# Two first expert products behind attention, later row turning, copies ahead of a square, another pair order

## The chip, the cores and the metric

The kernel runs on one core of a Trainium2 chip. The metric is the device time of one execution in microseconds (us), the median of several runs. The core has a matrix engine (TensorE, PE in the views; its weight loads are PEld), a vector engine (VectorE, DVE), a scalar engine (ScalarE, ACT), GpSimd (POOL), and SyncE (SP), which here does nothing but issue DMAs. Each engine executes its own instructions in order; engines meet through semaphores.

## What is computed

Attention without softmax over 8 batches of 2496 tokens, then a mixture of 8 experts, where each token goes to one expert and an expert keeps the 80 tokens of largest gate weight:

```python
scores = (1.0 / S) * np.matmul(z, z.transpose(0, 2, 1))   # z: 8 x 2496 x 64
attn = np.maximum(scores, 0.0) ** 2
x = u * np.matmul(attn, v)                                # u, v: 8 x 2496 x 256
logits = x.reshape(-1, 256) @ w_gate                      # 256 x 8
expert_idx = argmax(logits); gate_w = softmax(logits)[expert_idx]
for e in range(8):                                        # at most 80 tokens each
    h = np.maximum(x[tok_idx] @ w1[e], 0.0)               # w1: 256 x 1024
    out[tok_idx] = gate_w[tok_idx, None] * (h @ w2[e])    # w2: 1024 x 256
```

## The kernel before

**Tiles and stages.** Attention runs batch by batch. A batch has 5 chunks of queries (`qc` 0 to 4, 512 columns, the last 448) and 20 blocks of 128 keys, taken in 10 pairs. A step is one chunk with one pair (`r` 0 to 9 counts the steps of a chunk), so there are 8 x 5 x 10 steps. Products are made in two-part precision: a number is a high part (`ah`, a cast) and a low part (`al`, the difference, L58). A step has 24 accumulating products (L444, `acc`), and most of them also 6 score products (L407, `s`).

**Look ahead.** In step i the scores of step i+2 are issued: PE writes `s`, ACT takes the positive part (L409) and the square (L410), ACT or DVE casts `ah`, DVE makes `al` (L58). Scores are symmetric, so a block below the diagonal is not computed again: DVE turns it (L316, `x`), SP writes it to DRAM (L326, `y`) and later reads it back as `blk` (L343); then ACT casts it (L387) and DVE makes its `al`. Four slots hold such blocks. The diagonal's quarter goes the same way through `xd`, `yd` and `md`. The tables `pairs_of`, from `order()`, say in which order a chunk takes its pairs. In chunk 3 that is pair 6, 0, 8, 9, 1, 2, 3, 4, 5, 7; pairs 6 to 9 are scored, 0 to 5 are read back.

**The chain of a finished chunk.** When the ten pairs are summed in the two accumulators, `take` copies them (ACT, L516). In the steps of the following chunk DVE adds the first part of it (`chunk_add`, r=0), multiplies with `u` (`chunk_x`, L524, r=1), takes the rest (`chunk_rest`, r=3) and the low part (`chunk_lo`, tile `xl`, r=5); a store at r=4 (`chunk_store`), the gate logits (L602) at r=7 and their sum (L609) at r=8 end it. `CHAIN` holds these numbers. All of it stands in the same queues as the attention work of the next chunk.

**Rows for the experts.** The experts read tokens as rows, and `x` is kept as columns. In batches 0 and 1 each finished chunk is turned at once by two DMA transposes (L560) and written as rows (L568); from batch 2 on the chunk is stored to DRAM as it is (`xu`, L580).

**The end.** Behind the last chunk PE makes the first product of expert 0 (`first_product`, `hp_first`, L832), a count of tokens (`count`, L711), and the logits of the last chunk (L549, L553). The last `x` of attention is finished by `chunk_x_last` (ACT copies L538, DVE). Then each expert's products follow: `hp` (L832), the transposes `tp` (L1351), `op` (L1366). The experts' weights are split in high and low parts by ACT and DVE casts and subtractions (L911, L921), the first of them at the steps listed in `SPLITS`.

**What sets the order.** The program is issued in the written order under a manual schedule: the position of a call in the loop over the steps is the position in every engine's queue. SP issues all the DMAs of the loop, and a DMA that waits for its source or for a free slot holds everything behind it.

Of the kernel before, what the change touches and what calls it, by code (L numbers as in the profile page):

```python
# [25 lines left out]
def attn_moe_kernel(ctx, tc, zT, uT, v, wg, w1, w2, out, seq, cap):  # L26
# [30 lines left out]
    def tt(o, a, b, op):  # L57
        V.tensor_tensor(out=o, in0=a, in1=b, op=op)  # L58
# [36 lines left out]
    gt = dram.tile([NTOK, 1], F32, name="gt")  # L95
    xu = {(b, qc): dram.tile([P, DC, CH], F32, name=f"xu_{b}_{qc}") for b in range(2, B) for qc in range(NQ)}

# [293 lines left out]

    def scores(b, qc, k):
# [17 lines left out]
        nc.scalar.activation(out=a[:, :, c0:c1], in_=a[:, :, c0:c1], func=AF.Square)  # L410
        return lambda: split(b, qc, k, a, diag, lower, c0, nq)
# [86 lines left out]
    def top(x):  # L498
        return x.bitcast(BF16)[..., 1::2]

    def chunk_tiles(b, qc):
        xf = xpool.tile([P, 2, DC, CH], F32, tag="xf", name=f"xf_{b}_{qc}")

        xl = xpool.tile([P, DC, CH], BF16, tag="xl", name=f"xl_{b}_{qc}")
        nq = min(CH, seq - qc * CH)
        xt_t[b, qc] = [x[..., :nq] for x in (xf[:, 0], xf[:, 1], xl)]
        return xf[..., :nq]
# [67 lines left out]
    def chunk_store(b, qc):  # L575

        xf = xt_t[b, qc][0]
        nq = min(CH, seq - qc * CH)
        if b >= 2:
            nc.sync.dma_start(out=xu[b, qc][:, :, :nq], in_=xf)  # L580
        elif qc in (2, 3):
            xq = sqpool.tile([P, 2, QT * 2 * D], U16, tag="x", name=f"xq_{b}_{qc}")[:, 0]
            xq_t[b, qc] = x_turn(xf, xq, nq)
        else:
            xq = zpool.tile([P, QT * 2 * D], U16, tag="vraw", name=f"xq_{b}_{qc}", bufs=3)
            xq_t[b, qc] = x_turn(xf, xq, nq)

    def chunk_store2(b, qc):
        if b < 2:
            x_rows(b, qc, min(CH, seq - qc * CH), xq_t.pop((b, qc)))  # L590
# [394 lines left out]
    def weights_ahead(qc, r):  # L985
        if not places:
# [72 lines left out]
    ex_t = {}  # L1059
    CHAIN = 3, 5, 4, 6, 7, 8  # L1060

    with tc.manual_schedule(engines={ET.PE, ET.Activation, ET.DVE, ET.SP, ET.Pool}):
# [10 lines left out]
        for i, (b, qc, r) in enumerate(steps):  # L1073
# [239 lines left out]
    def ffn_of(own, num, expert, tw, to, ps_t, ps_h):  # L1313
# [66 lines left out]
    def ahead():  # L1380
        with ExitStack() as stack:
# [58 lines left out]
            with tc.manual_schedule(engines={ET.PE, ET.Activation, ET.DVE, ET.Pool}):  # L1440
# [3 lines left out]
                for i in range(E):  # L1444
# [7 lines left out]
                    if i + 1 < E:  # L1452
                        ffn_x(i + 1, xall[0][:, i + 1], V)
# [96 lines left out]
    with tc.If(nc.values_load(flag[0:1, 0:1], min_val=0, max_val=1) > 0):  # L1550
        for i in range(B * NQ):
            zero_out(i, B * NQ)
        with tc.tile_pool(name="gx", bufs=1) as gx:
# [55 lines left out]
```

## Time and profile before

| | us |
|---|---|
| median of 3 runs | 1342.36 (1341.12 to 1347.63) |
| the profiled execution | 1343.44 |
| its span in the trace | 1341.7 |
| PE busy | 1304.5 |
| DVE busy | 1060.9 |
| ACT busy | 1014.0 |
| share of the 16 DMA engines, main queue | 76.0% |

Names in the rows carry the program's names without buffer numbers. A timeline row is one or several like instructions of an engine that follow each other (`x4`): when the first began, how long from there to the end of the last, and in brackets how long the engine had been idle before and what released it. In the rows of a window, busy times stand with the number of instructions. Matmuls overlap, so that between two of full width that wait for nothing some 0.23 us pass from start to start although each is listed with 0.39.

Batches 3 to 7 take about 157 us each, from the first accumulating product of one to that of the next; batches 1 and 2 take 159.

### The profile page before, as it was taken

The numbers are of one execution on the slowest core, as the hardware profiler recorded it, in microseconds if no ns is written. First come the engines' busy times: TensorE is split into PE (matmuls) and PEld (weight loads), VectorE is DVE, ScalarE is ACT, GpSimd is POOL, SyncE is SP. The second block draws the span as 40 slices with busy tenths as digits, with TensorE's granted clock in tenths as the row PEclk, the third lists the DMA queues.
The fourth block names the chain that finished last, engine by engine and source line by source line (L and its number), as shares of the span: only waits on it lengthen the run. The fifth ranks groups of instructions, "written<-read, shape, count | busy, mean of one in ns | idle before, by whom it ended". The sixth has DMA issues, their size and how long they took to land.

```text
span 1341.7 us, 31268 instructions
## 1 busy us (share of the span) xinstructions
PE 1304.5 (97%) x13119; PEld 1071.5 (80%) x13119; DVE 1060.9 (79%) x1277; ACT 1014.0 (76%) x1102; POOL 43.3 (3%) x58
## 2 busy tenths in 40 slices
PE   9999899999999999999999999999999999999997
PEld 6887778778877788878888788887888788887886
DVE  7877698677887788787887688877887778877785
ACT  8976688766887578776887678876787768878765
POOL 0000000000001000000002000000000000003011
PEclk9999999999999999999999999999999999999989
DMA  6798978987877848969578877788579695689763
GB/s 209 255 285 246 244 225 245 266 235 223 256 242 228 242 156 244 277 189 267 163 236 251 247 206 219 225 262 229 164 237 262 200 264 168 216 252 260 220 217 120
DMA packets 192740, 306.98 MB, mean 229 GB/s; under 512 B 35872, under 2 KB 117712, under 8 KB 182352
## 3 DMA queue, kind: packets, MB, share of 16 engines
q1 hardware_dynamic: 191312, 302.62, 76.0%
q0 software_dynamic: 1280, 2.30, 0.6%
q8 instruction: 104, 1.70, 0.5%
q14 instruction: 44, 0.36, 0.1%
HBM read 163.66 MB, written 136.09 MB: 223 GB/s over the span
## 4 chain that ended last, share of the span: by engine, by line
PE 72%; DVE 8%; ACT 7%; DMA 7%; issue 4%; SPq 2%; POOL 0%; DVEq 0%; ACTq 0%; POOLq 0%
PE acc L444 57%; PE s L407 9%; DVE al L58 3%; DMA blk<-y 2%; ACT a L409 2%; DVE x L316 2%; ACT ah L114 2%; PE hp L832 1%; PE pl L602 1%; DMA md<-yd 1%; ACT a L410 1%; PE op L1366 1%; DMA zraw<-zT 1%; DVE xf L58 1%; ACT ah L387 1%
## 5 line engine op out<-in xcount | busy, mean ns | idle before, releaser
L444 PE MATMUL acc<-ah,vt 64*128 64x512 f32 (+1 forms) x6240 | 954.7, 383 | 5.7 <-ACT xf L516 5.3
L444 PEld LDWEIGHTS acc<-ah,vt 64*128 64x128 f32 x6240 | 586.7, 184 | 121.2 <-ACT xf L516 14.9
L444 PE MATMUL acc<-al,vt 64*128 64x512 f32 (+1 forms) x3120 | 614.4, 385 | 17.1 <-DVE al L58 16.5
L58 DVE TENSOR_TENSOR al<-a,ah 128x1024 fp32r<-128x1024 f32 (+1 forms) x240 | 271.0, 1129 | 143.9 <-ACT ah L114 141.2
L444 PEld LDWEIGHTS acc<-al,vt 64*128 64x128 f32 x3120 | 300.0, 184 | 86.8 <-DVE al L58 33.5
L409 ACT ACTIVATE a<-s 128x1024 f32<-128x1024 f32 x240 | 229.2, 955 | 137.8 <-PE s L407 112.9
L410 ACT ACTIVATE a<-a 128x1024 f32<-128x1024 f32 x240 | 238.1, 992 | 7.6
L387 ACT CAST ah<-blk 128x1024 fp32r<-128x1024 f32 x160 | 164.5, 1050 | 99.5 <-PE acc L444 93.2
L58 DVE TENSOR_TENSOR al<-blk,ah 128x1024 fp32r<-128x1024 f32 x160 | 193.6, 1221 | 46.5 <-ACT ah L387 43.8
L114 ACT CAST ah<-a 128x1024 fp32r<-128x1024 f32 (+3 forms) x217 | 213.4, 984 | 5.7
L316 DVE STREAM_TRANSPOSE x<-a 128x1024 f32<-128x1024 f32 x160 | 198.1, 1238 | 0.0
L58 DVE TENSOR_TENSOR xf<-xf 128x1024 f32<-128x1024 f32 (+1 forms) x78 | 91.9, 1178 | 0.0
L407 PE MATMUL s<-zh,zl 64*128 64x512 f32 x480 | 89.8, 371 | 0.0
L407 PE MATMUL s<-zl,zh 64*128 64x512 f32 x480 | 89.7, 370 | 0.0
L516 ACT COPY xf<-acc 128x1024 f32<-128x1024 f32 (+1 forms) x78 | 76.4, 994 | 15.0 <-PE acc L444 14.3
L407 PE MATMUL s<-zh,zh 64*128 64x512 f32 x320 | 63.4, 393 | 0.0
L58 DVE TENSOR_TENSOR al<-md,ah 128x512 fp32r<-128x512 f32 x37 | 25.1, 679 | 35.2 <-ACT ah L422 35.1
L407 PEld LDWEIGHTS s<-zl,zh 64*128 64x128 f32 x480 | 45.2, 185 | 8.4
L407 PEld LDWEIGHTS s<-zh,zl 64*128 64x128 f32 x480 | 45.4, 185 | 6.4
L147 DVE TENSOR_TENSOR vt<-vraw,vt 128x1024 fp32r<-128x1024 f32 x40 | 48.5, 1213 | 0.0
L524 DVE SCALAR_TENSOR_TENSOR xf<-xf,ut 128x1024 f32<-128x1024 f32 (+1 forms) x39 | 45.8, 1175 | 0.0
L58 DVE TENSOR_TENSOR xl<-xf 128x1024 bf16<-128x1024 f32 (+1 forms) x39 | 45.8, 1174 | 0.0
(190 smaller groups left out, 738.5 us busy)
## 6 DMA issues: line engine op xcount, KB each, us to landing
y<-x SPq DMA_DIRECT2D x80, 1024.0 KB
blk<-y SPq DMA_DIRECT2D x320, 256.0 KB
out<-idle SPq DMA_DIRECT2D x40, 512.0 KB
vraw<-v SPq DMA_DIRECT2D x32, 512.0 KB
ut<-uT SPq DMA_DIRECT2D x32, 512.0 KB
wraw<-w SPq DMA_DIRECT2D x30, 512.0 KB
xu<-xf SPq DMA_DIRECT2D x24, 512.0 KB
yd<-xd SPq DMA_DIRECT2D x37, 256.0 KB
```

The costliest lines, as they stand in the source:

```text
L58: V.tensor_tensor(out=o, in0=a, in1=b, op=op)
L114: eng.copy(out=o, in_=i)
L147: e1.tensor_tensor(out=vt[:, :, 1], in0=raw, in1=vt[:, :, 0], op=ALU.subtract)
L316: V.transpose(out=x[:, :, :, t:t + 2].rearrange("p n k t s -> p t k n s"), in_=a)
L387: nc.scalar.copy(out=natural(ah), in_=src)
L407: nc.tensor.matmul(s[:, h, c0:c1], zk[hs, t * P:(t + 1) * P], zq[hs], start=n == 0, stop=n == 2)
L409: nc.scalar.activation(out=a[:, :, c0:c1], in_=s[:, :, c0:c1], func=AF.Relu)
L410: nc.scalar.activation(out=a[:, :, c0:c1], in_=a[:, :, c0:c1], func=AF.Square)
L444: nc.tensor.matmul(acc_t[b, qc][c][:, h, :nq], v_t[b, k // QT][hs, k % QT, iv, c * P:(c + 1) * P], x[hs, k % 2, :nq], start=at not in begu ...
L516: nc.scalar.copy(out=x[:, :, c], in_=acc_t[b, qc][c][:, :, :x.shape[-1]])
L524: V.scalar_tensor_tensor(out=x[:, 0], in0=x[:, 0], scalar=CSQ, in1=u_t[b, qc][:, :, :x.shape[-1]], op0=ALU.mult, op1=ALU.mult)
L602: nc.tensor.matmul(to[:, h, t], xb[i % 3][hs, i // 3, t0:t0 + P], wgs[hs, i // 3], start=i == 0, stop=i == 3 * DC - 1)
```

## The change

Six edits are made together.

1. All chunks are stored to `xu`. Those of batches 0 and 1 are turned later: in chunks 0 and 1 of batches 2 to 6, one stored chunk each is loaded (r=1), turned by the same two DMA transposes (r=4) and written as rows (r=7), in buffers of `vraw`.
2. Chunk 3 takes its pairs in the order 6, 0, 1, 8, 9, 2, 3, 4, 5, 7.
3. At the last step of a batch the square of the pair scored there is issued behind the two copies of the finished chunk.
4. The low part of `x` is written into the low halves of the rest's own words; the tile `xl` goes.
5. In chunk 0 of a batch the chain of the finished chunk begins one step later (add at r=1, product with `u` at r=2, rest at r=4).
6. Behind attention the first products of experts 0 and 1 are made in a row (`hp_first`, `hp_second`), ahead of the logits and the count. The splits of expert 1's last weights move from steps 4, 5 and 6 of the last chunk to 6, 8 and 9.

```diff
-            rest = rest[:1] + rest[-2:] + rest[1:-2]
+            rest = rest[:2] + rest[-2:] + rest[2:-2]
...
+        if later:
+            return lambda: (square(), split(b, qc, k, a, diag, lower, c0, nq))
+        square()
...
-        tt(xl, xr, top(xr), ALU.subtract)
+        tt(xr.bitcast(BF16)[..., 0::2], xr, top(xr), ALU.subtract)
...
+        nc.sync.dma_start(out=xu[b, qc][:, :, :min(CH, seq - qc * CH)], in_=xf)
...
+    def turn(step):
+        b, qc = to_turn[0]
         nq = min(CH, seq - qc * CH)
-        if b >= 2:
-            nc.sync.dma_start(out=xu[b, qc][:, :, :nq], in_=xf)
...
+        if step == 0:
+            xt_t["turn"] = x = raw_tile(f"xt_{b}_{qc}")
+            nc.sync.dma_start(out=x[:, :, :nq], in_=xu[b, qc][:, :, :nq])
+        elif step == 1:
+            xq = raw_tile(f"xq_{b}_{qc}").rearrange("p c t -> p (c t)").bitcast(U16)
+            xq_t["turn"] = x_turn(xt_t.pop("turn"), xq, nq)
         else:
...
+            to_turn.pop(0)
+            x_rows(b, qc, nq, xq_t.pop("turn"))
...
+    def first_products():
...
+        x_t[1] = x_second
+        nc.scalar.copy(out=x_t[1][0], in_=xp[:, :DC * NS])
+        tt(x_t[1][1], xp[:, :DC * NS], x_t[1][0], ALU.subtract)
         hp = ps_s.tile([P, 2, CH], F32, tag="s", name="hp_first")
...
+        hp = ps_a.tile([P, 2, CH], F32, tag="acc", name="hp_second")
+        for part in range(2):
+            product1(hp[:, part], 1, 1, part, NS)
...
-    SPLITS = dict(zip([(qb, 2), (qb, 4), (qb, 6), (qb, 7), (qz, 2), (qz, 4), (qz, 5), (qz, 6)], early))
+    SPLITS = dict(zip([(qb, 2), (qb, 4), (qb, 6), (qb, 7), (qz, 2), (qz, 6), (qz, 8), (qz, 9)], early))
...
-                rest = scores(nb, nqc, 2 * pairs_of[nb, nqc][nr])
+                rest = scores(nb, nqc, 2 * pairs_of[nb, nqc][nr], r == NP - 1 and qc == NQ - 1)
...
-            if r == 0 and prev:
+            shift = 1 if qc == 0 else 0
+            if r == shift and prev:
                 chunk_add(*prev)
-            if r == (0 if last else 1) and prev:
+            if r == (0 if last else 1 + shift) and prev:
                 chunk_x(*prev)
...
+            if 2 <= b < B - 1 and qc < 2 and r in TURN:
+                turn(TURN.index(r))
...
-        h_first = first_product()
-        count(b, 0, BPB - 2, b)
+        first_products()
         split_rest()
         gate_near(b, 0)
         chunk_store(*prev)
         chunk_logits_last(*prev)
+        count(b, 0, BPB - 2, b)
...
-    CHAIN = 3, 5, 4, 6, 7, 8
+    TURN = 1, 4, 7
+    CHAIN = 3, 5, 4, 7, 8
```

Three places show how this stands in the engines' queues. In the names, `al_3_3_18` is batch 3, chunk 3, block 18 (the first block of pair 9), `xf_3_2` is the finished chunk 2 of batch 3, and the last number is a counter.

DVE at the start of chunk 3 of batch 3, before:

```order
L58 TENSOR_TENSOR al_3_3_0_8452<-blk_3_3_0_7933,ah_3_3_0_8450 128x1024
L58 TENSOR_TENSOR al_3_3_16_8465<-a_3_3_16_8454,ah_3_3_16_8464 128x1024
L316 STREAM_TRANSPOSE x_3_4_3_8468<-a_3_3_16_8454 128x2x4x4x32
L58 TENSOR_TENSOR xf_3_2_8434<-xf_3_2_8434 128x1024
L58 TENSOR_TENSOR al_3_3_18_8510<-a_3_3_18_8499,ah_3_3_18_8509 128x1024
L316 STREAM_TRANSPOSE x_3_4_3_8468<-a_3_3_18_8499 128x2x4x4x32
L524 SCALAR_TENSOR_TENSOR xf_3_2_8434<-xf_3_2_8434,ut_3_2_8197 128x1024
L58 TENSOR_TENSOR al_3_3_2_8543<-blk_3_3_0_7933,ah_3_3_2_8541 128x1024
```

and after the change:

```order
L58 TENSOR_TENSOR al_3_3_0_8438<-blk_3_3_0_7921,ah_3_3_0_8436 128x1024
L58 TENSOR_TENSOR al_3_3_2_8442<-blk_3_3_0_7921,ah_3_3_2_8440 128x1024
L58 TENSOR_TENSOR xf_3_2_8421<-xf_3_2_8421 128x1024
L58 TENSOR_TENSOR al_3_3_16_8489<-a_3_3_16_8478,ah_3_3_16_8488 128x1024
L316 STREAM_TRANSPOSE x_3_4_3_8492<-a_3_3_16_8478 128x2x4x4x32
L528 SCALAR_TENSOR_TENSOR xf_3_2_8421<-xf_3_2_8421,ut_3_2_8184 128x1024
L58 TENSOR_TENSOR al_3_3_18_8532<-a_3_3_18_8521,ah_3_3_18_8531 128x1024
L316 STREAM_TRANSPOSE x_3_4_3_8492<-a_3_3_18_8521 128x2x4x4x32
```

The subtraction for block 2 (pair 1), whose pair is now used third, stands ahead of the work for pairs 8 and 9.

ACT where batch 3 ends and batch 4 begins, before:

```order
L409 ACTIVATE a_4_0_4_9252<-s_4_0_4_9253 128x1024
L410 ACTIVATE a_4_0_4_9252<-a_4_0_4_9252 128x1024
L516 COPY xf_3_4_9274<-acc_3_4_0_8889 128x2x448
L516 COPY xf_3_4_9274<-acc_3_4_1_8890 128x2x448
L114 CAST ah_4_0_4_9284<-a_4_0_4_9252 128x1024
```

and after the change:

```order
L409 ACTIVATE a_4_0_4_9237<-s_4_0_4_9238 128x1024
L520 COPY xf_3_4_9258<-acc_3_4_0_8874 128x2x448
L520 COPY xf_3_4_9258<-acc_3_4_1_8875 128x2x448
L411 ACTIVATE a_4_0_4_9237<-a_4_0_4_9237 128x1024
L114 CAST ah_4_0_4_9268<-a_4_0_4_9237 128x1024
```

The copies that free the accumulators now stand one instruction earlier.

ACT at the end of attention, before:

```order
L647 ACTIVATE ex_last_203<-d_7_0_18167 128x128
L911 CAST w1h_2_51_18187<-wall_2_1_18002 128x1024 x2
L538 COPY xf_7_4_18191<-acc_7_4_0_17844 128x256
L538 COPY xf_7_4_18191<-acc_7_4_0_17844 128x192
L538 COPY xf_7_4_18191<-acc_7_4_1_17845 128x256
L538 COPY xf_7_4_18191<-acc_7_4_1_17845 128x192
```

and after the change:

```order
L657 ACTIVATE ex_last_213<-d_7_0_18164 128x128
L937 CAST w2h_1_49_18184<-wraw_1_2_0_17837 128x1024
L937 CAST w1h_2_51_18188<-wall_2_1_18003 128x1024
L937 CAST w2h_1_49_18184<-wraw_1_2_1_17971 128x1024
L937 CAST w1h_2_51_18188<-wall_2_1_18003 128x1024
L542 COPY xf_7_4_18194<-acc_7_4_0_17847 128x256
L542 COPY xf_7_4_18194<-acc_7_4_0_17847 128x192
L542 COPY xf_7_4_18194<-acc_7_4_1_17848 128x256
L542 COPY xf_7_4_18194<-acc_7_4_1_17848 128x192
L837 CAST x_second0_215<-xp_second_18238 128x224
```

Four casts of weights stand ahead of the last copies of `x` where two stood, and the cast for expert 1's first product stands behind them.

## Rows read from the trace of the kernel before

**Rows 1.** The page, part 1: busy us (share of the span), instructions.

```profile
PE 1304.5 (97%) x13119; PEld 1071.5 (80%) x13119; DVE 1060.9 (79%) x1277; ACT 1014.0 (76%) x1102; POOL 43.3 (3%) x58
```

**Rows 2.** Waits by releaser: engine, line, releaser: us in total, times, longest.

```profile
PE acc L444 <- DVE al L58: 16.5, 24, 3.0
...
PE acc L444 <- ACT xf L516: 5.3, 11, 0.8
```

**Rows 3.** Timeline of PE, chunk 3 of batch 3.

```profile
598.50 0.84 PE L444 MATMUL acc<-ah,vt 64*128 64x512 f32 x5
600.39 0.51 PE L444 MATMUL acc<-al,vt 64*128 64x512 f32 x2 [1.06 <-DVE al L58]
```

**Rows 4.** Timeline of DVE, same stretch.

```profile
599.12 2.35 DVE L58 TENSOR_TENSOR al<-blk,ah 128x1024 fp32r<-128x1024 f32 x2
```

**Rows 5.** Timeline of ACT, end of batch 3.

```profile
643.48 1.03 ACT L409 ACTIVATE a<-s 128x1024 f32<-128x1024 f32 x1 [1.00 <-PE s L407]
644.54 1.06 ACT L410 ACTIVATE a<-a 128x1024 f32<-128x1024 f32 x1
645.50 1.70 ACT L516 COPY xf<-acc 128x896 f32<-128x896 f32 x2
```

**Rows 6.** Timeline of PE, same stretch.

```profile
645.56 0.40 PE L407 MATMUL s<-zl,zh 64*128 64x512 f32 x2
646.44 0.73 PE L444 MATMUL acc<-ah,vt 64*128 64x512 f32 x4 [0.49 <-ACT xf L516]
```

**Rows 7.** Timeline of DVE, chunk 0 of batch 4.

```profile
653.59 1.05 DVE L58 TENSOR_TENSOR xf<-xf 128x896 f32<-128x896 f32 x1
...
656.49 1.23 DVE L58 TENSOR_TENSOR al<-a,ah 128x1024 fp32r<-128x1024 f32 x1
```

**Rows 8.** Timeline of PE, same stretch.

```profile
656.83 0.61 PE L444 MATMUL acc<-ah,vt 64*128 64x512 f32 x4
657.77 0.50 PE L444 MATMUL acc<-al,vt 64*128 64x512 f32 x2 [0.32 <-DVE al L58]
```

**Rows 9.** Timeline of DVE and PE, chunk 4 of batches 0 and 1.

```profile
158.18 0.43 DVE L122 CAST zh<-zraw 128x512 fp32r<-128x512 f32 x1 [5.45 <-DMA zraw<-zT]
...
161.66 0.47 PE L444 MATMUL acc<-al,vt 64*128 64x448 f32 x2 [3.04 <-DVE al L58]
...
320.66 0.47 PE L444 MATMUL acc<-al,vt 64*128 64x448 f32 x2 [1.12 <-DVE al L58]
```

**Rows 10.** Windows: stretch, length, busy time by engine, PE clock, DMA share, GB/s.

```profile
133.00:137.00 4.00, 4.00 (x82) 3.40 (x76) 1.16 (x2) 1.81 (x3) 0.00 (x0) 1.00 1.17 164
...
185.00:193.00 8.00, 8.00 (x74) 6.60 (x72) 7.81 (x7) 7.75 (x9) 0.00 (x0) 1.00 0.74 175
...
611.00:615.00 4.00, 4.00 (x80) 3.26 (x78) 1.89 (x3) 2.51 (x4) 0.00 (x0) 1.00 1.08 367
```

**Rows 11.** The page, part 5: group, count, busy us, mean ns, idle before.

```profile
L58 DVE TENSOR_TENSOR xf<-xf 128x1024 f32<-128x1024 f32 (+1 forms) x78 | 91.9, 1178 | 0.0
...
L58 DVE TENSOR_TENSOR xl<-xf 128x1024 bf16<-128x1024 f32 (+1 forms) x39 | 45.8, 1174 | 0.0
```

**Rows 12.** Timeline of ACT, end of attention.

```profile
1271.41 1.98 ACT L911 CAST w1h<-wall 128x1024 fp32r<-128x1024 f32 x2
1273.30 0.37 ACT L538 COPY xf<-acc 128x256 f32<-128x256 f32 x1
...
1275.62 0.32 ACT L538 COPY xf<-acc 128x192 f32<-128x192 f32 x1 [0.88 <-DVE xf L58]
```

**Rows 13.** Timeline of PE, end of attention and first experts.

```profile
1272.92 0.48 PE L832 MATMUL hp_first<-w1h,x_first 128*112 128x512 f32 x1
...
1276.94 1.93 PE L553 MATMUL pl<-wg_sb,xf 128*128 128x8 f32 x16
...
1287.23 0.27 PE L1366 MATMUL op<-w2h,hTh 128*112 128x256 f32 x1
```

**Rows 14.** Window of the same stretch, columns as in the other windows.

```profile
1279.40:1283.40 4.00, 3.35 (x9) 2.25 (x10) 3.63 (x12) 0.44 (x2) 1.03 (x1) 0.51 0.02 4
```

More of the change, by code (lines that the diff above doesn't have):

```diff
@@ L95, in attn_moe_kernel @@
     gt = dram.tile([NTOK, 1], F32, name="gt")
-    xu = {(b, qc): dram.tile([P, DC, CH], F32, name=f"xu_{b}_{qc}") for b in range(2, B) for qc in range(NQ)}
+    xu = {(b, qc): dram.tile([P, DC, CH], F32, name=f"xu_{b}_{qc}") for b in range(B) for qc in range(NQ)}
     wtab = dram.tile([(NBLK + 1) * E, 2 * P], BF16, name="wtab")
@@ L390, in mirrored, with scores @@
         a_t[b, qc, k] = (ah, al)
-    def scores(b, qc, k):
+    def scores(b, qc, k, later=False):
         if k // QT < qc:
@@ L409, in scores, with square @@
         nc.scalar.activation(out=a[:, :, c0:c1], in_=s[:, :, c0:c1], func=AF.Relu)
-        nc.scalar.activation(out=a[:, :, c0:c1], in_=a[:, :, c0:c1], func=AF.Square)
+        def square():
+            nc.scalar.activation(out=a[:, :, c0:c1], in_=a[:, :, c0:c1], func=AF.Square)
+        if later:
+            return lambda: (square(), split(b, qc, k, a, diag, lower, c0, nq))
+        square()
         return lambda: split(b, qc, k, a, diag, lower, c0, nq)
@@ L502, in chunk_tiles @@
         xf = xpool.tile([P, 2, DC, CH], F32, tag="xf", name=f"xf_{b}_{qc}")
-        xl = xpool.tile([P, DC, CH], BF16, tag="xl", name=f"xl_{b}_{qc}")
         nq = min(CH, seq - qc * CH)
-        xt_t[b, qc] = [x[..., :nq] for x in (xf[:, 0], xf[:, 1], xl)]
+        xt_t[b, qc] = [xf[:, i, :, :nq] for i in range(2)]
         return xf[..., :nq]
@@ L527, in chunk_rest @@
     def chunk_rest(b, qc):
-        xf, xr, _ = xt_t[b, qc]
+        xf, xr = xt_t[b, qc]
         tt(xr, xf, top(xf), ALU.subtract)
     def chunk_lo(b, qc):
-        _, xr, xl = xt_t[b, qc]
-        tt(xl, xr, top(xr), ALU.subtract)
+        xr = xt_t[b, qc][1]
+        tt(xr.bitcast(BF16)[..., 0::2], xr, top(xr), ALU.subtract)
     def chunk_x_last(b, qc, c):
@@ L577, in chunk_store, with raw_tile @@
         xf = xt_t[b, qc][0]
-        nq = min(CH, seq - qc * CH)
-        if b >= 2:
-            nc.sync.dma_start(out=xu[b, qc][:, :, :nq], in_=xf)
-        elif qc in (2, 3):
-            xq = sqpool.tile([P, 2, QT * 2 * D], U16, tag="x", name=f"xq_{b}_{qc}")[:, 0]
-            xq_t[b, qc] = x_turn(xf, xq, nq)
-        else:
[L585 to L590, printed above, removed]
+        nc.sync.dma_start(out=xu[b, qc][:, :, :min(CH, seq - qc * CH)], in_=xf)
+    to_turn = [(b, qc) for b in range(2) for qc in range(NQ)]
+    def raw_tile(name):
+        return zpool.tile([P, DC, CH], F32, tag="vraw", name=name, bufs=3)
+    def turn(step):
+        b, qc = to_turn[0]
+        nq = min(CH, seq - qc * CH)
+        if step == 0:
[4 more added lines that the diff above has]
+            xq_t["turn"] = x_turn(xt_t.pop("turn"), xq, nq)
+        else:
+            to_turn.pop(0)
+            x_rows(b, qc, nq, xq_t.pop("turn"))
     def chunk_logits(b, qc):
         nq = min(CH, seq - qc * CH)
-        xf, xr, xl = xt_t[b, qc]
-        xb = top(xf), top(xr), xl
+        xf, xr = xt_t[b, qc]
+        xb = top(xf), top(xr), xr.bitcast(BF16)[..., 0::2]
         pl = ps_m.tile([P, 2, CH], F32, tag="m", name=f"pl_{b}_{qc}")[:, :, :3 * QT * E]
@@ L706, in count @@
         kr = RB[b] * BPB + k0
-        tp = ps_m.tile([P, 2, CH], F32, tag="m", name=f"tp_{b}_{k0}")[:, :, :n * E]
+        pool, tag = (ps_a, "acc") if b == B - 1 else (ps_m, "m")
+        tp = pool.tile([P, 2, CH], F32, tag=tag, name=f"tp_{b}_{k0}")[:, :, :n * E]
         rows = [slice(0, P)] if b < 2 or b == B - 1 else HALVES
@@ L814, in first_x @@
         tt(xl, xp[:, :DC * NS], xh, ALU.subtract)
-    def first_product():
+    h_first = {}
+    x_second = [const.tile([P, DC * NS], F32R, name=f"x_second{i}") for i in range(2)]
+    def first_products():
+        one = vpool.tile([P, QT * 2 * D], F32, tag="vt", name="h_first")
+        xp = ps_m.tile([P, 2, CH], F32, tag="m", name="xp_second")[:, 0]
+        for c in range(DC):
+            nc.tensor.transpose(out=xp[:, c * NS:(c + 1) * NS], in_=xall[0][:NS, 1, c * P:(c + 1) * P],
+                                identity=ident[:NS, :NS])
+        x_t[1] = x_second
+        nc.scalar.copy(out=x_t[1][0], in_=xp[:, :DC * NS])
+        tt(x_t[1][1], xp[:, :DC * NS], x_t[1][0], ALU.subtract)
         hp = ps_s.tile([P, 2, CH], F32, tag="s", name="hp_first")
-        h = vpool.tile([P, QT * 2 * D], F32, tag="vt", name="h_first")
         for part in range(2):
             product1(hp[:, part], 0, 0, part, NS)
-        nc.scalar.activation(out=h[:NS, :F], in_=hp[:NS].rearrange("p a f -> p (a f)"), func=AF.Relu)
-        return h[:, :F]
+        h_first[0] = one[:, :F]
+        nc.scalar.activation(out=h_first[0][:NS], in_=hp[:NS].rearrange("p a f -> p (a f)"), func=AF.Relu)
+        hp = ps_a.tile([P, 2, CH], F32, tag="acc", name="hp_second")
+        for part in range(2):
+            product1(hp[:, part], 1, 1, part, NS)
+        h_first[1] = vpool.tile([P, QT * 2 * D], F32, tag="vt", name="h_second")[:, :F]
+        nc.scalar.activation(out=h_first[1][:NS], in_=hp[:NS].rearrange("p a f -> p (a f)"), func=AF.Relu)
     def product1(hp, i, e, part, ns):
@@ L992, in weights_ahead @@
             places.extend([xt, xt, xt, vv, a4[1], vv, a4[2], vv, a4[3], vv])
-            places.extend([None, None, None, vv, a4[0], 1])
+            places.extend([None, None, None, a4[0], 1])
         if (qc, r) in SPLITS:
@@ L1022, in finished @@
         at_end = b == B - 1 and qc == NQ - 2
-        rest, lo, store, store2, logits, total = (1, 3, 3, 5, 5, 6) if at_end else CHAIN
+        rest, lo, store, logits, total = (1, 3, 3, 5, 6) if at_end else CHAIN
         if qc == NQ - 1:
-            logits, total = 7, 8
+            rest = 4
         if r == rest:
@@ L1031, in finished @@
             chunk_store(b, qc)
-        if r == store2:
-            chunk_store2(b, qc)
         if r == logits:
@@ L1157, in attn_moe_kernel @@
         gate_rows(b, ex_last, gp, nc.gpsimd)
-        chunk_store2(*prev)
     main.close()
@@ L1330, in ffn1 @@
             ns = num(i)
-            if not own and i == 0:
-                h_t[i] = h_first
+            if not own and i in h_first:
+                h_t[i] = h_first[i]
                 return
@@ L1451, in ahead @@
                         ffn_h(0, 1)
-                    if i + 1 < E:
+                    if i + 1 < E and i + 1 not in x_t:
                         ffn_x(i + 1, xall[0][:, i + 1], V)
@@ L1565, in attn_moe_kernel @@
             with tc.tile_pool(name="gxu", bufs=2) as gxu:
-                for b, qc in xu:
+                for b, qc in [at for at in xu if at[0] >= 2]:
                     nq = min(CH, seq - qc * CH)
```

## The prediction, on record before the changed kernel ran

> **What bounds the kernel now.** I read the page's first part, then the waits, then the timelines where PE waits. PE is busy 97% of the span and DVE 79% [rows 1]: the kernel is bound by PE, and what a change can give is PE's idle time plus work taken from PE. In the attention part nearly all idle time of accumulating products has two releasers: the low parts from DVE, 16.5 us in 24 waits, and the copies of a finished chunk on ACT, 5.3 us in 11 [rows 2]. Together 21.8 us, a ceiling for edits 1 to 5. The reader is to see that the waits are few and come back at fixed places of a batch; each is priced below from start to start of two matmuls, less the 0.23 us that pass anyway.
>
> **Edit 2, chunk 3's order.** The last of five `ah` products begins 0.39 before the end of its row, at 598.95, and the next product begins at 600.39 [rows 3]: 1.44, a stall of 1.21. It waits for the first `al` of pair 1 on DVE, begun at 599.12 in a row of two that takes 2.35 us [rows 4]. DVE reaches it so late because it works off two scored pairs, their turns and two pieces of the `x` chain in the same two steps. The new order has pair 1's `al` ahead of all that, so its operand lies ready two steps earlier. The pairs then late are 8 and 9, each one step later than before on PE too, with the same DVE work in front less the two `al` of pair 1. By the old durations they are ready about 0.4 us before use. Chunk 3 stands like this in 7 batches: 7 x 1.21 = 8.5 us gained. If the slack of 0.4 isn't there, a stall of the same size moves to pair 8 and nothing is gained; that is in the rivals. On SP the read of the next block no longer stands behind that late `al`'s slot, so SP is freed earlier, which costs nothing.
>
> **Edit 3, copies ahead of the square.** ACT ends the positive part at 644.51, squares until 645.60 and copies from 645.50, 0.85 for each of the two [rows 5]. PE finishes starting its scores at 645.56 and gets the accumulator at 646.44 [rows 6]: 0.88, a stall of 0.65. With the copies first, the first is done at 644.55 + 0.85 = 645.4, before PE asks. Gain 7 x 0.65 = 4.6. The square and the cast of that pair come 1.7 us later. That pair is used two steps, over 6 us, later, so nobody waits.
>
> **Edit 5, x a pair later in chunk 0.** PE begins its last `ah` product at 657.05 and the next at 657.77 [rows 8], a stall of 0.48 in 7 batches. Its `al` is begun at 656.49, and the addition to `xf`, 1.05 us, stands three places ahead of it [rows 7]. Moved behind, it makes `al` 1.05 earlier, but PE itself arrives 0.65 earlier by edit 3, so 0.48 + 0.65 = 1.13 are needed and 1.05 are there. I take edits 3 and 5 together as 7 x 1.05 = 7.3. The three later pieces go into steps of 3.4 us in which DVE has one `al` (1.2) and one turn (1.2), so a third piece of 1.2 just fits: cover is thin, 7 x 0.3 are the price if it is not enough.
>
> **Edit 1, turns moved.** In chunk 4 of batches 0 and 1 PE waited 3.04 and 1.12 us for an `al` that stood on DVE behind a cast waiting 5.45 us for `zraw` [rows 9]. Start to start these are stalls of 3.2 and 1.3. At the same step of the later batches, which store and don't turn, no such wait shows. While the two transposes of that stretch were in flight the DMA engines were full (1.17) at 164 GB/s, where the same place of batch 3 moved 367 GB/s at 1.08 [rows 10]. So both go: 4.5 us. The ten turns reappear in chunks 0 and 1 of batches 2 to 6, with one load and one store of 512 KB more each. Their nearest row is the same operation at the same step: batch 1 issued two transposes at 185, chunk 0, r=4, and PE was busy 8.00 of the next 8.00 us at a DMA share of 0.74 [rows 10]. By that row a turn costs nothing; the far bound is the 3.2 us of the stall above, each. A gain beyond is excluded, since no PE work goes. I take 0.05 each, 0.5 in all, being nearest to that row, and keep the far end as a rival.
> By those windows a turned byte costs the queue about twice a copied one. The Trainium skill, Advanced Engine Details and Errata, section X-Bar Transpose (TRN2), says the opposite: transposing DMAs are as fast as regular ones. By that rule a store in place of a turn frees nothing and the 4.5 would be 0.
>
> **Edit 4, low parts in place.** The subtraction is 1174 ns to a packed tile; the one that reads alternate halves has 1178 [rows 11], so reading strided costs nothing, and strided writing is not in the trace. From both sides: a gain is excluded, since the same elements pass; at most, by analogy with a second pass, 1.2 us more on DVE at r=5. I take 0, by the reading row.
>
> **Edit 6, the end.** Before, `hp_first` begins at 1272.92 and `op` of expert 0 at 1287.23 [rows 13], 14.3 us. After, expert 1's product (2.8 us at full clock, as `hp_first`) comes ahead. But four casts stand on ACT where two took 1.98 [rows 12], so the last copies of `x` end at 1275.94 + 1.9 = 1277.85, and the cast for `hp_second` 0.4 later. PE ends `hp_first` at 1276.1, idles to 1278.3, ends `hp_second` at 1281.1. Logits take 1.93 [rows 13] and the count 0.2: 1283.3. Behind them PE waits for DVE, which has two subtractions of weights (1.2 each) and six small gate steps in front of what it needs, and then for two casts of the transposed `h`: some 4.7, so `op` begins at 1288.0, 0.8 later. Expert 1's own transposed low part then stands behind more of DVE's weight work: 0.8 more. The clock was granted at 0.51 in 1279.4 to 1283.4 [rows 14], that is 1.2 GHz, after PE had idled three times; a like stretch will now fall on `op` or behind it, 0 to 2.8 more. I take +2.5 in all, with +5 and, if every wait there vanished, -5.2 as ends (2.8 of work at half clock saved and 2.4 of idle).
>
> **Sum.** -8.5 - 7.3 - 4.5 + 0.5 + 2.5 = -17.3. The profiled execution took 1343.44 us with a span of 1341.7, 1.1 above the median of 1342.36. 1343.44 - 17.3 - 1.1 gives 1325.0, against the median.
>
> **Rivals.**
> *Given back at the next wait, 1333.* Pairs 8 and 9 come late in chunk 3, the shifted `x` pieces crowd DVE, or the strided write is slow. For: slacks of 0.1 and 0.4 us are worked out with before's durations. Against: DVE idles a fifth of the span. Half of 15.8 is lost, 7.9 more: 1333, within 1330 to 1337.
> *Turns hold the DMA queue, 1356.* Slower than before. Each of the ten turns now stands in the middle of a batch on SP ahead of blocks that PE needs; if each costs 3.2 as in chunk 4 of batch 0 [rows 9], it is 32 in place of 0.5: 1325 + 31.5 = 1356.5. It decides from (17.3 + 0.5) / 10 = 1.8 us per turn. Against: batch 1's window at the same step with PE full [rows 10].
> *Turning is no dearer than copying, 1329.5.* Then the wait for `zraw` stays with a store in place of the turn: 4.5 back. Against: the two windows [rows 10].
> *The end fills PE, 1317.* The casts on ACT come early enough, PE doesn't idle between the two products, and the clock stays: -5.2 in place of +2.5. For: 2.8 us of PE work are there to fill the gap. Against: the cast's place in ACT's queue.
> *The end loses the clock longer, 1330.* If both `op` of expert 0 (2.8 at full clock) and `hp` of expert 2 run at 1.2 GHz, it is +7.5 in place of +2.5. For: more short bursts with waits between. The Trainium skill, TensorE: Matmul & The Clock Gate, section HAM oscillation, says that bursts broken by waits put the clock back to half rate each time; the stretch at 0.51 agrees.
>
> **How the numbers follow.** Forecast 0.55, itself 1320 to 1330; given back 0.18; the two rivals near 1330 together 0.12; the end fills PE 0.07; turns cost between nothing and 1.8, so that no change shows, 0.04; turns slower 0.04. The range 1314 to 1336 takes in the forecast, the rivals at 1329.5, 1330 and 1317 and most of the given-back case, and leaves out some 0.13. Within 0.5%, which is about what a measurement of this kernel can tell from no change, is above 1335.6: a fifth of the given-back case and the 0.04 make 0.09 with some allowance, slower 0.04, faster 0.87.
>
> **What would show it.** In the changed profile: in chunk 3 no wait of PE above 0.5 us at the third pair (edit 2); at a batch's start PE follows its scores at once (edit 3); at the fourth pair of chunk 0 a wait below 0.2 (edit 5); batches 1 and 2 as long as the later ones, all near 155 us (edits 1 to 5); no wait for `zraw` over 2 us; next to the turns, PE full as at 185; the group of in-place low parts near 1174 ns; `op` of expert 0 about 15 us behind `hp_first`. I am wrong if batches 3 to 7 stay at 157, if the ones with turns are longer than batch 7, or if the end is over 5 us longer.

## The result and the profile after

| | before | changed |
|---|---|---|
| median, us | 1343.63 (4 runs) | 1327.20 (4 runs) |
| ratio, 95% interval | | 0.9875 [0.9847, 0.9903] |
| the profiled execution, its span | 1343.44, 1341.7 | 1328.22, 1326.5 |

The change gains 16.4 us, by the interval 13 to 21. Forecast were 17.3 and 1325.0.

The first part of the profile's page after, and then the waits of PE (engine, line, releaser: us in total, times, longest), which answer to [rows 1, 2]:

```profile
PE 1300.0 (98%) x13119; PEld 1074.3 (81%) x13119; DVE 1063.0 (80%) x1276; ACT 1017.0 (77%) x1102; POOL 42.8 (3%) x58
```

```profile
PE s L407 <- ACT a L409: 4.9, 8, 1.1
PE acc L449 <- DVE al L58: 4.0, 12, 0.5
...
PE tp L1378 <- DVE d_last L58: 2.3, 1, 2.3
PE hp_second L858 <- ACT x_second L837: 2.0, 1, 2.0
...
PE acc L449 <- ACT xf L520: 1.0, 2, 0.8
```

The waits for low parts fell from 16.5 us to 4.0 and those for the copies from 5.3 to 1.0. But a wait that edits 1 to 5 were not meant to touch has grown, from 1.1 us in one: scores that wait for ACT, 4.9 us in 8 waits. Two more are new at the end.

It helps to cut each trace in two at the last accumulating product of attention. Both lengths are read from PE's timeline; attention counts from its first accumulating product, whose own start varies by a microsecond from run to run.

| profiled execution | attention, us | end, us |
|---|---|---|
| before | 1261.9 | 68.7 |
| changed | 1243.7 | 72.6 |

So attention gained 18.2 us and the end lost 3.9.

**Chunk 3.** Timeline of PE, changed kernel, chunk 3 of batch 5, where the third pair (now pair 1, which was the fifth before) gives way to the fourth; the answer to [rows 3]:

```profile
895.14 0.39 PE L449 MATMUL acc<-al,vt 64*128 64x512 f32 x2
895.37 0.62 PE L449 MATMUL acc<-ah,vt 64*128 64x512 f32 x4
895.83 0.39 PE L449 MATMUL acc<-al,vt 64*128 64x512 f32 x2
```

No row has a bracket: PE runs through, and the profile lists no wait of PE in the whole chunk. Chunks 2 and 3 of batch 5 together shrank by 1.43 us. They are taken together because the new order also moves 0.68 us of score products across their border.

**A batch's first steps.** Timeline of ACT and then of PE, changed kernel, end of batch 4; the answer to [rows 5, 6]:

```profile
786.15 1.03 ACT L409 ACTIVATE a<-s 128x1024 f32<-128x1024 f32 x1 [1.01 <-PE s L407]
787.15 1.73 ACT L520 COPY xf<-acc 128x896 f32<-128x896 f32 x2
788.78 1.06 ACT L411 ACTIVATE a<-a 128x1024 f32<-128x1024 f32 x1
789.87 1.05 ACT L114 CAST ah<-a 128x1024 fp32r<-128x1024 f32 x1
790.83 1.02 ACT L409 ACTIVATE a<-s 128x1024 f32<-128x1024 f32 x1
```

```profile
788.23 0.40 PE L407 MATMUL s<-zl,zh 64*128 64x512 f32 x2
788.47 0.62 PE L449 MATMUL acc<-ah,vt 64*128 64x512 f32 x4
...
791.89 0.50 PE L407 MATMUL s<-zh,zh 64*128 64x512 f32 x2 [0.54 <-ACT a L409]
```

The accumulating product follows the scores after 0.24 us, as forecast. One step later PE stops before its scores: it waits for the positive part that ACT begins at 790.83, behind the two copies, the square and the cast. The stall is 791.89 less the last product's start at 790.97, less 0.23: 0.69 us, and the gain was 0.65.

That positive part does not come later than it did. The row of ACT that follows [rows 5] in the kernel before:

```profile
648.03 1.04 ACT L409 ACTIVATE a<-s 128x1024 f32<-128x1024 f32 x1
```

It begins 2.5 us behind PE's last scores at 645.56 [rows 6], and after the change 2.6 behind those at 788.23. Square, copies and cast stand in front of it in either order; edit 3 only brought PE to the wait sooner.

**The turns.** SP and two windows of the changed kernel, batch 5, chunk 0 and chunk 1, each with a turn in it, issued at 806.21 and 838.31 (first the issue, then length, busy times, PE clock, DMA share, GB/s):

```profile
806.21 4.28 SPq L564 DMA_TRANSPOSE xq<-xt  x2
```

```profile
806.00:814.00 8.00, 8.00 (x78) 6.64 (x76) 7.92 (x9) 7.79 (x9) 0.00 (x0) 1.00 1.14 216
838.00:846.00 8.00, 8.00 (x80) 6.46 (x78) 7.83 (x12) 7.17 (x8) 0.00 (x0) 1.00 1.07 319
```

PE is full beside them, as in the row of batch 1 [rows 10]. Chunk 1 of batches 3 to 6 takes 32.6 to 32.7 us in both kernels, so a turn costs PE nothing there.

**The end.** Timeline of ACT, then of PE, then windows of the changed kernel; the answers to [rows 12 to 14]:

```profile
1255.15 1.04 ACT L937 CAST w1h<-wall 128x1024 fp32r<-128x1024 f32 x1
1256.10 0.35 ACT L542 COPY xf<-acc 128x256 f32<-128x256 f32 x1
...
1258.63 0.35 ACT L837 CAST x_second<-xp_second 128x224 fp32r<-128x224 f32 x1
```

```profile
1254.00 0.46 PE L858 MATMUL hp_first<-w1h,x_first 128*112 128x512 f32 x1
...
1259.03 0.48 PE L858 MATMUL hp_second<-w1h,x_second 128*112 128x512 f32 x1 [2.03 <-ACT x_second L837]
...
1267.86 1.73 PE L1378 MATMUL tp<-ident,h_first 112*128 112x112 f32 x8 [2.33 <-DVE d_last L58]
...
1270.22 0.54 PE L1393 MATMUL op<-w2h,hTh 128*112 128x256 f32 x1
```

```profile
1261.80:1265.80 4.00, 3.72 (x23) 2.83 (x21) 0.93 (x4) 2.54 (x3) 0.00 (x0) 0.75 1.01 357
...
1269.80:1273.80 4.00, 3.82 (x22) 3.76 (x21) 3.62 (x18) 3.19 (x4) 1.07 (x4) 0.50 0.63 234
```

The reader sees both waits at the places where the prediction had put them, and the clock at 0.50, that is 1.2 GHz, over most of the 24 products of `op`. They take from 1270.22 to 1274.83, 4.6 us, where the kernel before took 2.8. Behind them both kernels need another 51.5 us to their end, so all that the end lost lies ahead of that point.

### The profile page after: what moved, and what is told of

The parts are those of the page before. It is cut to its first block, busy times and chain, and to the rows that moved or that the text cites. A ratio compares the mean times of both kernels' runs of the same rounds, so it can differ in the third digit from the quotient of the medians.

```text
span 1326.5 us, 31268 instructions
## 1 busy us (share of the span) xinstructions
PE 1300.0 (98%) x13119; PEld 1074.3 (81%) x13119; DVE 1063.0 (80%) x1276; ACT 1017.0 (77%) x1102; POOL 42.8 (3%) x58
## 4 chain that ended last, share of the span: by engine, by line
PE 76%; DMA 8%; ACT 6%; DVE 4%; issue 3%; SPq 2%; POOL 0%; POOLq 0%; DVEq 0%; ACTq 0%
PE acc L449 61%; PE s L407 10%; DMA blk<-y 3%; DMA y<-x 3%; DVE al L58 2%; ACT a L409 2%; PE pl L612 2%; ACT a L411 1%; PE op L1393 1%; ACT xf L520 1%; PE hp L858 1%; SPq L343 1%; ACT ah L387 1%; DMA zraw<-zT 1%; DMA vraw<-v 1%
## 5 line engine op out<-in xcount | busy, mean ns | idle before, releaser
L58 DVE TENSOR_TENSOR xf<-xf 128x1024 f32<-128x1024 f32 (+3 forms) x117 | 144.5, 1235 | 0.0
L528 DVE SCALAR_TENSOR_TENSOR xf<-xf,ut 128x1024 f32<-128x1024 f32 (+1 forms) x39 | 45.8, 1174 | 0.0
L407 PEld LDWEIGHTS s<-zh,zh 64*128 64x128 f32 x320 | 30.1, 184 | 12.2 <-ACT a L409 6.7
```

Of the source, the lines that this page charges most:

```text
L528: V.scalar_tensor_tensor(out=x[:, 0], in0=x[:, 0], scalar=CSQ, in1=u_t[b, qc][:, :, :x.shape[-1]], op0=ALU.mult, op1=ALU.mult)
```

## The experiments

The kernels ran on three chips (e1 to e4 on one, e5 to e8 on another, e10 to e13 on a third), each beside the kernel before on the same chip; so ratios are compared, and the lengths of the two parts. The kernel before took 1346.28, 1341.54 and 1342.39 us on them. On the chip of e1 to e4 chunk 2 of batch 4 took 34.4 to 34.5 us in all four, where it takes 31.5 elsewhere (32.2 with the old order of chunk 3); 3.0 us (in e3 2.3) are taken off their attention below. The times that were expected of e1 to e4 did not have these 3 us in them.

| kernel | median, us | ratio, 95% interval | attention, us | end, us |
|---|---|---|---|---|
| e13, the changed kernel again | 1327.49 | 0.9892 [0.9876, 0.9909] | 1243.5 | 70.8 |
| e1, edit 6 undone | 1326.46 | 0.9852 [0.9833, 0.9871] | 1243.3 | 67.5 |
| e2, edit 3 undone | 1330.63 | 0.9883 [0.9864, 0.9901] | 1243.1 | 71.1 |
| e3, edit 2 undone | 1339.66 | 0.9947 [0.9926, 0.9968] | 1255.1 | 70.5 |
| e4, edit 5 undone | 1336.75 | 0.9928 [0.9910, 0.9946] | 1248.8 | 71.9 |
| e5, edit 1 undone | 1327.75 | 0.9901 [0.9885, 0.9918] | 1243.2 | 70.6 |
| e6, one cast on DVE | 1321.23 | 0.9850 [0.9833, 0.9866] | 1236.9 | 72.5 |
| e7, second x early | 1326.63 | 0.9887 [0.9870, 0.9903] | 1242.9 | 70.5 |
| e8, e6 and edit 6 undone | 1318.32 | 0.9829 [0.9813, 0.9846] | 1237.9 | 68.5 |
| e10, e8 and edit 4 undone | 1318.32 | 0.9823 [0.9806, 0.9841] | 1238.1 | 68.5 |
| e11, edit 2 alone | 1329.63 | 0.9910 [0.9888, 0.9931] | 1248.3 | 68.6 |
| e12, edit 1 alone | 1338.01 | 0.9972 [0.9962, 0.9982] | 1257.5 | 67.5 |

**e1: the end as it was.**

```diff
-        first_products()
+        h_first = first_product()
+        count(b, 0, BPB - 2, b)
...
-        count(b, 0, BPB - 2, b)
```

> The changed kernel with edit 6 alone undone (one first product behind attention, the count ahead of the logits, the splits at their old steps). Theory: the end lost time, since the profiled execution of the changed kernel took 72.6 us from the last accumulating product to its end where the kernel before took 68.7; then attention stays at 1243.7 us, the end goes back to 68.7, and the time is 1323.5 to 1325. Rival: the longer end comes of attention's earlier finish (weights and rows not yet there), then the end stays near 72 and the time near 1327.

The end took 67.5 us and attention was unchanged. The seven traces with edit 6's own end have 70.5 to 72.6, the six with the old one (before among them) 67.5 to 68.7: edit 6 costs about 3 us. On one chip e6 and e8, which differ in edit 6 alone, are 2.9 us apart in their medians. The theory holds.

**e2: the square first.**

```diff
-                rest = scores(nb, nqc, 2 * pairs_of[nb, nqc][nr], r == NP - 1 and qc == NQ - 1)
+                rest = scores(nb, nqc, 2 * pairs_of[nb, nqc][nr])
```

> The changed kernel with edit 3 alone undone (the square stands ahead of the two copies again at the end of each batch). Theory: the stall of 0.65 us at a batch's first accumulating product was only moved to the scores of its second step, which wait 0.92 from start to start for ACT's positive part; undone, the first stall is back, the second gone, and the time stays at 1326 to 1328 with batches 3 to 6 at 154.6 to 155.2. Rival (the forecast): the copies ahead of the square gain 0.65 in each of 7 batches, and the time is 1331 to 1333.

The stall at the batch's first product is back (this kernel's PE timeline, batch 5, here on the other side of the chunk's border):

```profile
791.88 0.73 PE L449 MATMUL acc<-ah,vt 64*128 64x512 f32 x4 [0.49 <-ACT xf L520]
```

In exchange chunk 0 fell from 33.22 to 32.55 us, chunk 4 rose from 27.6 to 28.2, and attention is the same. Edit 3 gave nothing. The median of 1330.63 is near the rival's 1331, but 3.0 of it are this chip's; the ratio, 0.9883, is the changed kernel's.

**e3: the old order in chunk 3.**

```diff
-            rest = rest[:2] + rest[-2:] + rest[2:-2]
+            rest = rest[:1] + rest[-2:] + rest[1:-2]
```

> The changed kernel with edit 2 alone undone (chunk 3 takes pairs 8 and 9 ahead of pair 1 again). Theory: the order gained 1.43 us in each of 7 batches, as the steps of batch 5 show (chunks 2 and 3 together), so the time is 1336 to 1338. By the forecast's 1.21 it is 1335.5. Rival: another edit has taken the load off DVE there as well, the stall would be smaller now, and the time is below 1333.

Attention is 11.4 us longer than the changed kernel's, the ratio 0.0055 to 0.0072 higher (7 to 10 us). The order's own gain of about 10 holds; the rival, under 1333, falls. Of the 11.4 us, 1.4 are a stall that came up in chunk 4 of batch 2, behind a `zraw` that DVE awaited for 3.7 us.

**e4: no shift in chunk 0.**

```diff
-            rest = 4
+            rest = 3
...
-            shift = 1 if qc == 0 else 0
-            if r == shift and prev:
+            if r == 0 and prev:
...
-            if r == (0 if last else 1 + shift) and prev:
+            if r == (0 if last else 1) and prev:
```

> The changed kernel with edit 5 alone undone (the chain of the finished chunk begins at step 0 of chunk 0 again). Theory: the step of the fourth pair in chunk 0 grows by 0.63 us in 7 batches, as it had before, so the time is 1330.5 to 1331.5. Rival: edit 3 already gives DVE or PE 0.67 at the second step, the low part of the fourth pair is in time without the shift, and the time stays at 1326 to 1328.

Chunk 0 took 33.96 instead of 33.22 in every batch from 1 on: 0.74 each, 5.2 in all. That it is longer than in the kernel before (33.21) is the stall of 0.69 that edit 3 moved into it from chunk 4; the two chunks together took 61.1 to 61.6 us before, in batches 2 to 6, and 61.5 to 61.8 here. The mechanism holds and the size is a little over what was expected.

**e5: turned at once.**

```diff
-    TURN = 1, 4, 7
-    CHAIN = 3, 5, 4, 7, 8
+    CHAIN = 3, 5, 4, 6, 7, 8
...
-            if 2 <= b < B - 1 and qc < 2 and r in TURN:
-                turn(TURN.index(r))
```

> The changed kernel with edit 1 alone undone (chunks of batches 0 and 1 turned as soon as they are finished, none in later batches). Theory: the two stalls behind the late zraw come back, 3.2 and 1.3 us in chunk 4 of batches 0 and 1, and chunks 0 and 1 of batches 2 to 6 keep their lengths (33.2 and 32.6 us) since the turns there cost nothing: ratio to the kernel before 0.9875 + 0.0033 = 0.991. Rival: the ten turns cost something where they are, then batches 2 to 6 get shorter and the ratio is below 0.989.

Half of the theory fell. Chunks 0 and 1 of batches 2 to 6 kept their lengths, so the turns cost nothing there. But of the stalls only 0.5 us in batch 0 came back: chunk 4 of batches 0 and 1 took 28.2 and 27.6 us, where the kernel before took 31.2 and 29.7. Something other than the moved turns had ended them, and e11 and e12 ask what.

**e6: one cast on DVE.**

```diff
-    ON_V = {(0, 8)}
+    ON_V = {(0, 4), (0, 8)}
```

> The changed kernel with one thing more: in chunk 0 of every batch but the first, the high part of pair 2 is cast by DVE (0.65 us, where DVE had been idle 1.77) and no longer by ACT (1.05). Theory: what gave edit 3's gain back is ACT's queue in front of the next positive part (copies, square, cast); one cast less there ends the 0.92 wait of the scores at the second step, chunk 0 shrinks from 33.22 to about 32.55 us in 7 batches, and the ratio to the kernel before goes from 0.9875 to 0.984. Rival: the stall moves on once more, to the low part of pair 4 (which has 0.49 us left), and the ratio stays within 0.9865 to 0.9885.

Timelines of ACT, DVE and PE of this kernel at the end of batch 4:

```profile
784.73 1.06 ACT L411 ACTIVATE a<-a 128x1024 f32<-128x1024 f32 x1
785.69 1.02 ACT L409 ACTIVATE a<-s 128x1024 f32<-128x1024 f32 x1
```

```profile
785.82 0.69 DVE L116 CAST ah<-a 128x1024 fp32r<-128x1024 f32 x1 [0.68 <-ACT a L411]
```

```profile
786.92 0.39 PE L449 MATMUL acc<-al,vt 64*128 64x512 f32 x2
787.15 0.39 PE L407 MATMUL s<-zh,zh 64*128 64x512 f32 x2
```

ACT's positive part now follows its square at once, and PE's scores follow without a bracket. Chunk 0 shrank to 32.43 us, attention to 1236.9. So it was ACT's queue that had taken edit 3's gain back.

**e7: the second x early.**

```diff
+        second_x()      # transposes, cast and low part of expert 1's rows
         for kk, c in ((3, 0), (2, 0), (3, 1), (1, 0), (2, 1), (1, 1)):
```

> The changed kernel with expert 1's rows turned and cast ahead of the last copies of x, not behind them. Theory: PE's idle time of 2.03 us between the first products of experts 0 and 1 is ACT's queue; it goes, the second product begins at once, the logits begin when the last x is there, some 3 us sooner, and the end shrinks from 72.6 to 69 or 70 us: ratio 0.985. Rival: the end is set by DVE's and ACT's weight work behind the logits, and stays within 1 us of 72.6 (ratio 0.987).

PE's timeline of this kernel:

```profile
1258.16 0.46 PE L860 MATMUL hp_second<-w1h,x_second 128*112 128x512 f32 x1 [0.96 <-DVE xf L58]
...
1267.55 0.53 PE L1396 MATMUL op<-w2h,hTh 128*112 128x256 f32 x1
```

The wait fell from 2.03 to 0.96 and `op` began 13.3 us behind attention, where the seven traces with edit 6's own end have 14.4 to 16.3. But its products then took 5.4 us at the lower clock, and the end is 70.5, within the spread that one and the same end shows (70.5 to 72.6). That ACT's queue made half of the first wait is shown; that its removal shortens the end is not.

**e8: both.** The diffs of e1 and e6 together.

> The changed kernel with edit 6 undone and with pair 2's high part in chunk 0 cast by DVE. Theory: both gains add, 0.9852 for the end undone and 0.0035 for the cast, ratio 0.982. Rival: the cast gives nothing, ratio 0.985.

Attention has e6's gain to within 1 us, and the end is back among the old ones. The ratio is 0.9829, so the gains add.

**e10: low parts in a tile of their own.**

```diff
-        tt(xr.bitcast(BF16)[..., 0::2], xr, top(xr), ALU.subtract)
+        tt(xl, xr, top(xr), ALU.subtract)
```

> The kernel of e8 (edit 6 undone, pair 2's high part in chunk 0 on DVE) with edit 4 undone too: low parts go to a packed tile of their own again. Theory: the strided write takes DVE 1.35 us where the packed one took 1.17, and work beside it hides that 0.18, so the chunks keep the lengths of e8 within 0.1 us each and the ratio to the kernel before is 0.982 to 0.984. Rival: the 0.18 stands in PE's way in each of 39 chunks, then it is up to 7 us faster, ratio 0.978.

No difference to e8, so the longer instruction is hidden. Level with e8, this is also the fastest kernel found: 1318.32 us, 9 us under the changed kernel on the same chip (1327.49) and 24 under the kernel before (1342.39).

**e11 and e12: one edit alone, on the kernel before.** The diffs are that of edit 2 and that of edit 1.

> The kernel before with edit 2 alone (chunk 3's order). Theory: beside its own 1.43 us in 7 batches the order frees SP, which before stood 11 us on a read that waited for a slot; so zraw is issued some 4 us sooner in chunk 4 and the stalls of 3.2 and 1.3 us in batches 0 and 1 go too though the turns are still there: 14.4 us in all, ratio 0.989. Rival (the forecast): those two stalls come of the turns and stay, 10.0 us, ratio 0.9925.

> The kernel before with edit 1 alone (all chunks stored, those of batches 0 and 1 turned in batches 2 to 6). Theory: it takes the other half of the cause, the transposes in front of zraw, away, and also ends those two stalls by itself, while the ten turns cost nothing: 3 to 4.4 us less, ratio 0.997. Rival: the turns cost what they gain, ratio 1.0 or more.

> The changed kernel as it is, on the chip of this call, so that the others stand beside it. Both theories of the other runs put it at 0.9875 to 0.989 of the kernel before: by the theory that edit 2 alone ends the stalls of batches 0 and 1 its attention part is 4 to 5 us shorter than that of edit 2 alone, the share of edit 5 (0.66 in 7 batches); by the rival it is 9 us shorter.

Chunk 4 of batches 0 and 1, with chunks 2 and 3 of batch 5 for the order's own part (in the changed kernel chunk 4 is 0.65 shorter than 28.2 because edit 3 moves a stall across its border):

| | chunk 4, batch 0 | chunk 4, batch 1 | chunks 2 and 3, batch 5 |
|---|---|---|---|
| before | 31.2 | 29.7 | 62.6 |
| e12, edit 1 alone | 28.2 | 28.2 | 62.6 |
| e11, edit 2 alone | 29.6 | 28.2 | 61.2 |
| changed | 27.6 | 27.6 | 61.2 |

Edit 1 alone takes 2.9 and 1.4 us off the two stalls. Edit 2 alone takes 1.6 and 1.4 off, with the turns where they were. The ratio of e11 does not decide between its theory and the rival, since its interval holds both; the chunks do. SP and DVE of e11 show how:

```profile
113.87 2.72 SPq L343 DMA_DIRECT2D blk<-y  x4
...
145.51 0.75 SPq L109 DMA_DIRECT2D zraw<-zT  x1
```

```profile
154.96 0.43 DVE L122 CAST zh<-zraw 128x512 fp32r<-128x512 f32 x1 [3.48 <-DMA zraw<-zT]
```

In the kernel before, the same read of blocks was issued at 121.87, behind an SP that stood waiting, `zraw` at 149.28, and the cast began at 158.18 [rows 9]. In e11 all of that is 3 to 8 us earlier. There PE too reaches chunk 4 of batch 0 sooner, by 1.6 us, so the cast, 3.2 us earlier, gains 1.6 on it, and 1.2 us of that stall stay.

Edit 1 works at another place of the same queue. SP at r=4 of chunk 3 of batch 0, in the kernel before, then in e12:

```profile
128.63 5.86 SPq L560 DMA_TRANSPOSE xq<-xf  x2
134.53 0.59 SPq L157 DMA_DIRECT2D ut<-uT  x1
```

```profile
128.01 0.34 SPq L578 DMA_DIRECT2D xu<-xf  x1
130.12 0.40 SPq L157 DMA_DIRECT2D ut<-uT  x1
...
144.99 0.35 SPq L109 DMA_DIRECT2D zraw<-zT  x1
```

The block read in front is issued at the same time in both (121.87 and 121.81). SP spends 5.86 us on issuing the two transposes and 0.34 on the store; what follows comes 4.4 us earlier in e12, `zraw` 4.3, and the cast 4.5 (153.70). From its issue to its cast `zraw` takes 8.9 us before and 8.7 in e12, so the turns delayed its issue and hardly its landing. Whether the issue takes so long because the DMA engines work slowly on transposes was not separated.

So two things made the `zraw` of batches 0 and 1 late: transposes in the queue, and an SP held up by a slot. Each edit takes one away. That both are needed for such a stall is not shown: in e3, with no transpose near, `zraw` came late enough in chunk 4 of batch 2 to stall PE for 1.4 us.

The attention part of e13 is 4.8 us shorter than that of e11, the share of edit 5, as the theory had it.

## Why the prediction was right, point by point

- **What bounds.** The ceiling of 21.8 us held: attention gained 18.2 to 18.4. It was not a hard bound, since idle times in brackets are shorter than stalls from start to start (0.49 against 0.65 at a batch's first product): with e6 attention is 25.0 us shorter than before.
- **Edit 2, forecast 8.5.** Measured 13.6 alone (e11): 10.0 of its own (7 x 1.43; the stall itself is 1.21 to 1.22 in each of the 7 batches, as forecast, and the rest are smaller gaps) and 3.0 in chunk 4 of batches 0 and 1, the rest small. The step that failed is "SP is freed earlier, which costs nothing": it had a part in another stall.
- **Edit 3, forecast 4.6.** Measured 0 (e2). The failed step is "that pair is used two steps later, so nobody waits". It followed the pair's own operand and forgot what queues behind it on ACT: the next positive part, for which PE's next scores wait, and which no order of the same instructions in front of it brings forward. This is the rival of gains given back, in one place, and e6 shows the place.
- **Edit 5, in 7.3 with edit 3.** Measured 4.6 for both, all of it edit 5's. The cover that was called thin held.
- **Edit 1, forecast 4.5 less 0.5.** Right in size alone (4.4, e12), and right that the turns cost nothing where they went. The way to it was another than forecast: `zraw` was not long in landing among slowly moved bytes, SP issued it late. In the whole attention is within half a microsecond with edit 1 or without it (e5), since edit 2 had already taken most of the stall. The sum did not suffer, as it had that stall once: edits 1 and 2 together were forecast 12.5 and measured 13.6 (18.2 less the 4.6 of edits 3 and 5).
  Signs named ahead were missed. The changed kernel still has three waits of DVE for `zraw`. The longest, 3.7 us, is for the first read of the program and was there before (3.8); one of 2.7 in chunk 4 of batch 3 is over the 2 us that were named, and PE stalls 0.4 us behind it. Batch 2 took 157.5 us, not 155, and is longer than batch 7 (155.8), which was to mean that turns cost time. But without turns (e5) it took 157.3, so it is not the turns.
  The rule of the Trainium skill on transposing DMAs (Advanced Engine Details and Errata, X-Bar Transpose (TRN2)) would have given 0 for edit 1 alone. e12 measured 4.4, so a turn was not as cheap as a store at this place; that is one case and not a rate, and what it shows is SP's time to issue.
- **Edit 4, forecast 0.** Right (e10), though the instruction did get longer: its group stands at 1377 ns, not near 1174, another sign missed. Reading in strides was no measure for writing in strides.
- **Edit 6, forecast +2.5.** Measured about +3. Both waits were where they had been put; the second product began 5.0 us behind the first (forecast 5.4), `op` 16.2 (forecast 15.1), the half clock lay on `op`. Over all traces `op` begins some 1.5 us later than with the old end and takes some 1.7 longer; the 0.8 for expert 1's own low part does not show. In three of the seven (changed kernel, e4, e6) the clock already fell in `hp_second`, which then took 4.3 to 4.6 us in place of 3.0; these three have the longest ends, 71.9 to 72.6.
- **Sum.** -17.3 forecast; -13.6 - 4.6 + 3 is -15.2, and the medians say -16.4 and, on another chip, -14.9. Edits 3 and 5 were 2.7 too high, edits 1 and 2 together 1.1 too low, and edit 6 cost 0.5 more. That the total came out closer than its terms is luck in part.

## What to carry to other kernels

When an instruction is moved behind others on an in-order engine, follow not only its own result but the next thing that engine has to free for the bottleneck; the stall of 0.65 us moved by one step and stayed, since the queue up to that next thing held the same work as before. When two edits each remove one of the causes of a stall, their gains don't add (13.6 and 4.4 alone, 13.6 together): price them together. An SP that stands on a full slot, or takes long over an issue, delays everything behind it, and its price may appear later under another name: here the read was issued at 121.87 and PE stalled at 161.66.

## What was not expected of the hardware

The subtraction with alternate 2-byte elements as its output, written into the tile that it reads, took longer than the one with a packed output, though reading alternate halves cost nothing [rows 11]. Groups of DVE by shape, first the kernel before, then the changed one (count, busy us, mean ns, idle before):

```profile
L58 DVE TENSOR_TENSOR xl<-xf 128x1024 bf16<-128x1024 f32 x32 | 38.4, 1200 | 0.0
```

```profile
L58 DVE TENSOR_TENSOR xf<-xf 128x1024 f32<-128x1024 f32 x64 | 77.4, 1209 | 0.0
...
L58 DVE TENSOR_TENSOR xf<-xf 128x1024 bf16<-128x1024 f32 x32 | 44.1, 1377 | 0.0
```

That is 1377 ns against 1200, 0.18 us more each.

On the chip of e1 to e4, matmuls in chunk 2 of batch 4 ran slower for some 6 us with a granted clock of 1.00. PE's timeline of e1:

```profile
727.16 1.13 PE L449 MATMUL acc<-ah,vt 64*128 64x512 f32 x4
```

A group of four takes 1.13 us there and 0.62 elsewhere. Slow rows make up about half of the 3.0 us; the rest is a wait for ACT's copies right behind them. It appeared at the same place in all four kernels traced on that chip and in no trace from another; its cause stays open.
